# A hand-planned FFT kernel: where a copied spectrum's next step stands in TensorE's order, and when the next layer's tables are loaded

## The chip, the cores and the metric

One core of a Trainium2 chip runs the whole program. The metric is the device time of one execution in microseconds (us). Of the kernel before there are three runs, with a median of 811.83 us, and one execution under the profiler.

## What is computed

The network applies two layers in turn, each twice: A, B, A, B on `x` of 2048 rows by 512 columns, all in float32.

```python
x = x + A(layernorm(x))     # irfft2(rfft2(x) * W): over both axes
x = x + B(layernorm(x))     # y = irfft(rfft(u, 2L) * rfft(K, 2L))[:L] + u * Dskip, per column, over the rows
x = x + A(layernorm(x))
x = x + B(layernorm(x))
# K[d, l] = Re sum_n C[d,n] * exp(dt[d] A[d,n] l) * dt[d] B[d,n]   (512 columns x 2048 steps, 128 states)
```

The kernel `K` and its spectrum are the same for both B layers, so they are computed once.

## The kernel before, in words

The Fourier transforms are matrix products in two steps, each with a small table, and with an elementwise step between. Layer B (`forward_b`, `group_b`, `inv_b`) works on halves of 256 columns, called e=0 and e=1, and on eight groups q=0 to 7 of frequencies in each half. For one half:

- `forward_b` (L795) normalizes, multiplies by the first table and sends the result through a DMA (L809) to the rows of a large SBUF buffer, `Y[:, 8192:]` for e=0 and `Ya` for e=1.
- `group_b` (L859) takes one group. It needs the spectrum of K for that group in a buffer `kh` (a ring of four). In most cases a DMA loads it from DRAM (L886). For e=1 of the first layer B it doesn't exist yet. There the group loads the half-transformed K (`yk`, L874, a ring of three) and a table (L875), TensorE makes the spectrum (L824, called by L878), ScalarE copies it to `kh` (L882), and a DMA on ScalarE's queue stores it to `khat` (L883) for the second layer B. I call this step K. Then comes step X: the spectrum of the signal (L824 again, called by L891), which reads neither `kh` nor the store. After it come the product on VectorE (L898), the sums on GpSimd (L904), the inverse step V on TensorE (L915) and the copy back on ScalarE (L924).
- `inv_b` (L927) loads the rows again, transposed, by a DMA within SBUF (L934), after all eight groups of its half, multiplies (L942) and adds to `x` (L948).

In the second half of layer B's groups (e=1) the loads of `inv_b` for e=0 run at the same time. Once they are through, `Y[:, 8192:]` is free, and the ring `G` there holds tables for the second layer A: `first_a(1, 0)` loads its two with L666 and L668, `group_a` for g=1 to 15 with L594 and L596. All these go through the queue of SyncE (SP), which issues in program order and stops at an instruction whose wait isn't over.

Ahead of all that, `turn_k` (L1186) does the first step of K's own transform in 16 pieces: it loads from `kd` (L1193), multiplies (L1208), and for each of two halves ScalarE copies out of PSUM (L1213) and issues a store to `yk` (L1216). Twelve pieces lie beside the computation of K in the first part of the program. The last four lie beside layer B's e=0 groups; there each half takes a PSUM buffer of kind x (of which there are four) and a buffer of ring `iy` (four, shared with `forward_b`).

The order of instructions on each engine comes from a planner, `Clock` (L195 to L398). Every function above is a generator, a piece, that yields what its next step needs: engines, buffers, events. The planner keeps a model of when each engine, buffer and transfer is free, takes the earliest step that is ready (within 0.1 us the one of lowest rank), lets it emit its instructions, and moves on. What it emits is a fixed program; on the chip each engine runs its own list in order, and semaphores hold back what is not ready. Four details matter here:

- After a step, the piece's next step is ready no earlier than the end of everything that the step emitted, landings of DMAs included (L390 and L392). The model of a landing is 2.0 us behind the bytes at a fixed rate (L39, L302).
- A yield that begins with "+" leaves that time as it was (L391): the next step counts from the step before.
- `emitted(key, n)` asks only that n events of that name are in the program already, whatever their time; `after(key, n)` also takes their time.
- `mark` notes an event at the end of the step in which it stands. `("turn", 1)` marked eight times lets the first K step of e=1 load.

```python
            if not (isinstance(needs, str) and needs[:1] == "+"):
                p[2] = end
```

Of the kernel before, what the change touches and what calls it, by code (L numbers as in the profile page):

```python
# [400 lines left out]
class Net:  # L401
# [185 lines left out]
    def group_a(self, g):  # L587

        nc = self.nc
        Y1 = self.folded(1, g // 4)[:, :, :, g % 4]  # L590
        yield "SP G", self.emitted(("loaded", 0, 0 if g < 4 else 1), 8)
        G = self.w("G", [128, 1798])
        ca = G[:, :768].rearrange("p (a b) -> p a b", a=6)
        nc.sync.dma_start(ca, self.io["cGa"][g])  # L594
        W = G[:, 768:1796].rearrange("p (r s f) -> p r s f", r=2, s=2)
        nc.sync.dma_start(G[:, 768:1798], self.io["W"][g])  # L596
        yield "PE p:t AB", self.after(("forward", 1), 16), self.emitted(("loaded", 0, 1), 8)
        p = self.psum("t")
        AB = self.w("AB", [128, 2, 258])
        self.fold_d(p, 1, g)  # L600
        yield "POOL"
        nc.gpsimd.memset(AB[:, :, 0:65:64], 0.0)
        yield "ACT"

        re, im = slice(0, 64), slice(64, 128)
        pc, ps = p[:, 0:256], p[:, 256:512]
        for lanes, i in ((re, 0), (im, 1)):
            nc.scalar.copy(AB[lanes, i, 0:64], pc[lanes, 0:64])
            nc.scalar.copy(AB[lanes, i, 65:257], pc[lanes, 64:256])
        nc.scalar.copy(AB[im, 0, 1:257], ps[re])  # L610
        nc.scalar.mul(AB[re, 1, 1:257], ps[im], -1.0)
        self.drop(p)
        yield "POOL V"
        V = self.w("V", [128, 2, 258])
        nc.gpsimd.tensor_tensor(V[:, 1, :257], AB[:, 0, :257], AB[:, 1, :257], op=OP.subtract)
        yield "+ DVE"
        nc.vector.tensor_tensor(V[:, 0, :257], AB[:, 0, :257], AB[:, 1, :257], op=OP.add)
        self.drop(AB)
        yield "PE p:x p:x"
        X = [self.psum("x")[:, :257] for sg in range(2)]  # L620
        for sg in range(2):
            nc.tensor.matmul(X[sg], ca[:, sg, :], V[:, sg, :257], start=True, stop=True)
        self.drop(V)
        yield "DVE t1a t2a"
        t1, t2 = (self.w(k, [128, 2, 258]) for k in ("t1a", "t2a"))
        for sg in range(2):
            nc.vector.tensor_tensor(t1[:, sg, :257], X[sg], W[:, 0, sg], op=OP.mult)
            nc.vector.scalar_tensor_tensor(t2[re, sg, :257], X[sg][im], -1.0, W[im, 1, sg], op0=OP.mult, op1=OP.mult)
            nc.vector.tensor_tensor(t2[im, sg, :257], X[sg][re], W[re, 1, sg], op=OP.mult)
        self.drop(*X)  # L630
        yield "POOL Za"
        Z = self.w("Za", [128, 2, 258])
        nc.gpsimd.tensor_tensor(Z[:, :, :257], t1[:, :, :257], t2[:, :, :257], op=OP.add)
        self.drop(t1, t2)
        yield "PE p:h tp"
        tp = self.w("tp", [128, 2, 64])
        v = self.psum("h").rearrange("p (b m) -> p b m", b=4)
        H = [ca[:, 2 + 2 * sg:4 + 2 * sg, :].rearrange("p r (s c u) -> p r s c u", s=16, c=2)[:, :, :, 0] for sg in range(2)]
        for b in range(2):
            for sg in range(2):  # L640
                for r, o in ((0, 65 * b), (1, 65 * b + 1 - b)):
                    nc.tensor.matmul(v[64 * r:64 * r + 64, b], Z[:, sg, o:o + 64], ca[:, 2 + 2 * sg + r, :],
                                     start=sg == 0, stop=sg == 1)
        for sg in range(2):
            nc.tensor.matmul(v[:, 2 + sg], Z[:, sg, 129:257], H[sg], start=True, stop=True)
        self.drop(Z, G)
        yield "ACT", self.emitted(("fold", 1), g // 4 * 4)
        nc.scalar.copy(Y1[:, 0:2], v[:, 0:2].rearrange("p b (s m) -> p b s m", s=16))
        P, M = (v[:, 2 + sg].rearrange("p (r s u) -> p r s u", r=2, s=16) for sg in range(2))
        yc, ys = Y1[:, 2:4, :, 0:4], Y1[:, 2:4, :, 4:8]  # L650
        tp = tp.rearrange("p r (s u) -> p r s u", s=16)
        nc.scalar.copy(tp, P)
        yield "DVE"
        nc.vector.tensor_tensor(yc, tp, M, op=OP.add)
        nc.vector.tensor_tensor(ys[:, 0], M[:, 1], tp[:, 1], op=OP.subtract)
        nc.vector.tensor_tensor(ys[:, 1], tp[:, 0], M[:, 0], op=OP.subtract)
        self.mark("group", 1)

    def first_a(self, r, g):

        nc = self.nc
        Y1 = self.folded(r, g // 4)[:, :, :, g % 4]
        yield "SP G", self.emitted(("loaded", 0, 0), 8) if r else self.after(("norm", 0), 16)
        G = self.w("G", [128, 1284])
        ca = G[:, :768].rearrange("p (a b) -> p a b", a=6)
        nc.sync.dma_start(ca, self.io["cPa"][g])  # L666
# [192 lines left out]
    def group_b(self, r, q, e):  # L859
# [10 lines left out]
        kh = self.w(ring, [128, 2, 2, 256])  # L870
        self.mark("kh")
        if new:
            y, gk = self.w("yk", [128, 2, 2, 256]), self.w("gk", [128, 2, 4, 32])
            nc.sync.dma_start(y.rearrange("p g h d -> p g (h d)"), self.yk[1, two].rearrange("g c a b h d -> (c a b) g (h d)"))  # L874
            nc.sync.dma_start(gk, self.io["cGk"][q])  # L875
            yield "PE p:x p:x"
            K = [self.psum("x") for _ in range(2)]
            self.spectrum(gk, [y[:, j] for j in range(2)], K)  # L878
            self.drop(gk, y)
            yield "ACT"  # L880
            for j in range(2):
                nc.scalar.copy(kh[:, j].rearrange("p r d -> p (r d)"), K[j])  # L882
            nc.scalar.dma_start(self.khat[:, two, :, d], kh)  # L883
            self.drop(*K)
        else:
            nc.sync.dma_start(kh, self.khat[:, two, :, d])  # L886
        Y = self.place[e][:, two].rearrange("p g (h d) -> p g h d", h=2)
# [298 lines left out]
    def turn_k(self, q, i):  # L1186

        nc = self.nc
        kd = self.kd[q].rearrange("j (a s) d -> a j (s d)", s=16)
        last = q == 3  # L1190
        yield "SP yk" if last else "SP KT", self.after(("stored", q))
        KT = self.w("yk" if last else "KT", [128, 4, 128])
        nc.sync.dma_start(KT, kd[:, :, 128 * i:128 * i + 128])  # L1193
        if i == 0:
            yield "SP gk" if last else "SP sk"
            sk = self.w("gk" if last else "sk", [1, 128])
            nc.sync.dma_start(sk, self.io["B_Dskip"].rearrange("(q a d) -> q a d", q=4, a=1)[q])
            yield "DVE"
            o = KT[0:1, :, 0:32]
            nc.vector.tensor_tensor(o, o, sk.rearrange("p (j d) -> p j d", j=4), op=OP.add)  # L1200
        yield "PE p:x p:x" if last else "PE p:k"
        if last:
            p = [self.psum("x") for _ in range(2)]
        else:
            p = self.psum("k")
            p = p[:, :512], p[:, 512:]
        for h in range(2):
            nc.tensor.matmul(p[h], self.Rk[:, h, :], KT.rearrange("p j m -> p (j m)"), start=True, stop=True)  # L1208
        self.drop(KT)
        for h in range(2):  # L1210
            yield "ACT iy" if last else "ACT yh"
            r = self.w("iy" if last else "yh", [128, 4, 128])
            nc.scalar.copy(r.rearrange("p s (j d) -> p s j d", j=4), p[h].rearrange("p (j s d) -> p s j d", j=4, s=4))  # L1213
            if last:
                self.drop(p[h])
            nc.scalar.dma_start(self.yk[q // 2, :, :, :, i, h, 128 * (q % 2):128 * (q % 2) + 128]  # L1216
                                .rearrange("g c a d -> (g c) a d"), r)
            self.drop(r)
        self.mark("turn", q // 2)

    def plan_k(self):
# [195 lines left out]
```

## Time and profile before

| | us |
|---|---|
| three runs: lowest, median, highest | 807.78, 811.83, 815.23 |
| the profiled execution | 816.34 |
| its span, first to last instruction | 814.5 |

The span falls into parts, by the first and last instructions of the lines: the computation of K and the first layer A up to about 360 us; layer B, half e=0, to about 439 us; half e=1 to 512 us; then its inverse step, the second layer A to about 690 us, and the second layer B to the end. A row of the timeline reads: start in us, duration, engine, line, operation, output and input, count, and in brackets the idle time before it and what ended it. A row of the stage view reads: the stage, its length, busy time of TensorE's matmuls and weight loads, of VectorE, ScalarE and GpSimd, then the granted clock, the DMA engines' share and the rate. A row of the waits reads: who waited for whom, us in total, times, longest.

### The profile page before, as it was taken

The page shows a single profiled execution, that of the slowest core. Times are in us where ns is not written, and L with a number is a line of the kernel's source. Part 1 is how long each engine was busy: PE and PEld are TensorE (multiplying, and loading weights), DVE is VectorE, ACT ScalarE, POOL GpSimd, SP SyncE. Part 2 cuts the span into 40 slices and gives each one's busy share as a digit, 9 for nine tenths or more (in the row PEclk, how much of TensorE's full clock was granted, in tenths as well). Part 3 has the DMA queues.
Part 4 walks back from the last instruction along what each step waited for, and adds up shares of the span by engine and source line. Part 5 has one row for each costly group of instructions (what it writes and reads, how often), then busy time and mean ns, then how long its engine had stood idle before and what let it go on. Part 6 is the DMA issues. An engine that isn't in the chain of part 4 may idle for free. (4 is left out here: it accounts for less than half of the span.)

```text
span 814.5 us, 23463 instructions
## 1 busy us (share of the span) xinstructions
PE 657.6 (81%) x9892; PEld 421.9 (52%) x9892; DVE 511.9 (63%) x1019; ACT 423.7 (52%) x771; POOL 308.3 (38%) x339
## 2 busy tenths in 40 slices
PE   4388888778799898798778776899887898788896
PEld 4377555445556443346323542677765554444565
DVE  5957477947947684973333624686777598375632
ACT  5676898878877667744234132266543233423120
POOL 4381345625615231400323134255443454074520
PEclk9699899989899999999898988999998899989999
DMA  9424312531524844369967984710665424765938
GB/s 331 143 79 134 108 46 99 169 97 67 173 64 161 282 131 142 126 230 219 273 175 203 290 267 177 204 50 1 225 215 175 145 55 105 171 183 149 280 87 277
DMA packets 87544, 132.51 MB, mean 163 GB/s; under 512 B 5804, under 2 KB 59824, under 8 KB 86800
## 3 DMA queue, kind: packets, MB, share of 16 engines
q1 hardware_dynamic: 53008, 93.26, 37.7%
q10 hardware_dynamic: 34432, 37.76, 16.5%
q8 instruction: 78, 1.28, 0.7%
q14 instruction: 26, 0.21, 0.1%
HBM read 70.31 MB, written 27.13 MB: 120 GB/s over the span
## 5 line engine op out<-in xcount | busy, mean ns | idle before, releaser
L1151 POOL TENSOR_TENSOR Y<-wk,Y 128x1024 f32<-128x1024 f32 x32 | 66.2, 2069 | 116.3 <-issue 64.8
L904 POOL TENSOR_TENSOR wk<-wk 128x512 f32<-128x512 f32 x32 | 40.0, 1275 | 124.1 <-DVE wk L898 97.3
L898 DVE TENSOR_TENSOR wk<-ps,Y 128x512 f32<-128x512 f32 x64 | 39.5, 683 | 54.4 <-DMA Y<-khat 14.7
L942 PE MATMUL ps<-wk,cRbT 64*128 64x256 f32 x512 | 61.9, 384 | 7.1 <-DVE x L948 2.6
L793 ACT COPY wk<-ps 128x512 f32<-128x512 f32 x64 | 37.0, 587 | 57.9 <-PE ps L791 45.6
L791 PE MATMUL ps<-wk,cRb 128*32 128x256 f32 x1024 | 61.8, 388 | 5.5 <-DVE wk L514 3.1
L1136 DVE SCALAR_TENSOR_TENSOR wk<-wk,ps 128x1024 f32<-128x1024 f32 x32 | 38.9, 1216 | 38.6 <-ACT wk L1134 38.5
L942 PEld LDWEIGHTS ps<-wk,cRbT 64*128 64x128 f32 x512 | 51.7, 187 | 17.4 <-issue 7.2
L557 PE MATMUL ps<-cRa,wk 128*128 128x256 f32 x128 | 37.9, 423 | 27.6 <-POOL wk L539 26.8
L915 PE MATMUL ps<-wk,Y 32*32 32x256 f32 x1344 | 41.2, 433 | 21.1 <-POOL wk L904 13.4
L898 DVE TENSOR_TENSOR Y<-ps,wk 128x512 f32<-128x512 f32 x64 | 39.6, 683 | 27.0 <-issue 19.9
L1104 PE MATMUL ps<-wk,Y 96*128 96x512 bf16 x128 | 42.0, 412 | 17.0 <-DMA yk<-wk 7.1
L948 DVE TENSOR_TENSOR x<-x,ps 128x256 f32<-128x256 f32 x64 | 24.9, 409 | 48.6 <-PE ps L942 48.5
L791 PEld LDWEIGHTS ps<-wk,cRb 128*32 128x32 f32 x1024 | 37.9, 111 | 30.6 <-issue 5.7
L1120 ACT ACTIVATE Y<-ps 128x1024 f32<-128x1024 f32 x48 | 46.1, 1027 | 8.5 <-PE ps L1104 8.3
L924 ACT COPY Ya<-ps 128x256 f32<-128x256 f32 x64 | 19.4, 385 | 57.7 <-PE ps L915 44.5
L740 PE MATMUL ps<-cDaT,apart 128*32 128x256 f32 (+1 forms) x256 | 47.3, 333 | 1.4 <-DVE x L768 1.2
L1147 DVE TENSOR_TENSOR Y<-ps,Y 128x1024 f32<-128x1024 f32 x32 | 39.0, 1219 | 13.6 <-ACT ps L1140 13.5
L1164 PEld LDWEIGHTS ps<-Y 128*32 128x32 f32 x2048 | 34.4, 120 | 23.4 <-issue 15.4
L539 POOL TENSOR_TENSOR wk<-wk 128x256 f32<-128x256 f32 x32 | 27.1, 846 | 51.0 <-ACT wk L512 45.2
L904 POOL TENSOR_TENSOR wk<-Y 128x512 f32<-128x512 f32 x22 | 27.5, 1278 | 46.9 <-DVE Y L898 42.7
L1164 PE MATMUL ps<-Y 128*32 128x64 f32 x2048 | 39.7, 236 | 6.6 <-ACT wk L744 4.8
(216 smaller groups left out, 1668.9 us busy)
## 6 DMA issues: line engine op xcount, KB each, us to landing
yk<-wk ACTq DMA_DIRECT2D x32, 256.0 KB, 2.7
wk<-khat SPq DMA_DIRECT2D x16, 512.0 KB, 7.4
Y<-in_W_dram SPq DMA_DIRECT2D x12, 515.0 KB, 4.4
x<-in_cPa_dram SPq DMA_DIRECT2D x16, 384.0 KB, 3.5
Y<-in_cGa_dram SPq DMA_DIRECT2D x12, 384.0 KB, 3.1
x<-in_W_dram SPq DMA_DIRECT2D x16, 258.0 KB, 3.8
x<-in_A_x_dram SPq DMA_DIRECT2D x8, 512.0 KB, 6.9
kd<-wk SPq DMA_DIRECT2D x4, 1024.0 KB, 9.7
```

The lines of the kernel that those rows point to most:

```text
L740: nc.tensor.matmul(p[32 * i:32 * i + 32, o:o + n], self.folded(r, i)[:, b, s2].rearrange("p g m -> p (g m)"), self.DaT[:, b, first:first + ...
L791: self.nc.tensor.matmul(p[o:o + 32, 256 * h:256 * h + 256], self.Rb[:, 2 * h + j, 32 * a:32 * a + 32], xn[s], start=True, stop=True)
L898: nc.vector.tensor_tensor(t[c][:, j], x, kh[:, j, ::-1, :] if c else kh[:, j], op=OP.mult)
L904: nc.gpsimd.tensor_tensor(Z[:, :, c], t[0][:, :, c], t[1][:, :, c], op=op)
L915: nc.tensor.matmul(v[j][h][i:i + 32], gi[o:o + 32, j, 4 + 2 * s + c, :], Z[o:o + 32, j, c, :], start=c == 0, stop=c == 1)
L942: nc.tensor.matmul(q[s], self.RbT[o, i, :], y[o, i, :], start=i == 0, stop=i == 3)
L1104: self.nc.tensor.matmul(p, f[:, c:c + 128], self.oh[:k, o:o + 512], start=True, stop=True)
L1120: nc.scalar.activation(m[:, :, 1024:] if i == 2 else m[:, i, :1024], p.rearrange("p (i m) -> p i m", i=2) if i == 2 else p, AF.Exp)
L1136: nc.vector.scalar_tensor_tensor(s, c, MAGIC, p, op0=OP.subtract, op1=OP.subtract)
L1147: nc.vector.tensor_tensor(E[:, 1, :1024], p, m[:, :1024], op=OP.mult)
L1151: nc.gpsimd.tensor_tensor(E[:, 0, :1024], c, m[:, :1024], op=OP.mult)
L1164: nc.tensor.matmul(pk[32 * j:32 * j + 32, 64 * e:64 * e + 64], E1[:, r, i, :], E2[:, r, i], start=r == 0, stop=r == 1)
```

## The change

Three edits. The first two concern when steps become ready in the planner; the third the order of loads. No computation, transfer or buffer is added or taken away.

1. In `group_b`, a `yield "+"` behind the store to `khat`. Step X of the group is then ready from the end of step K's matmuls on, where it was ready from the landing of the store on.
2. In `turn_k`, a `yield "+"` behind each store to `yk`. The second half's copy is ready from the end of the matmuls on, where it waited for the first half's landing. The mark of the event `turn`, too, now carries the time of the matmuls' end. The semaphores on the chip still wait for the stores.
3. The first four table sets of the second layer A (`first_a(1, 0)` and `group_a` for g=1, 2, 3) wait until 16 `kh` buffers have been taken, so until the loads of the last group of e=1 are in the program. Before, they waited for eight `loaded` events, so for the last load of `inv_b` for e=0.

```diff
@@ group_a
-        yield "SP G", self.emitted(("loaded", 0, 0 if g < 4 else 1), 8)
+        yield "SP G", (self.emitted("kh", 16) if g < 4 else self.emitted(("loaded", 0, 1), 8))
@@ first_a
-        yield "SP G", self.emitted(("loaded", 0, 0), 8) if r else self.after(("norm", 0), 16)
+        yield "SP G", self.emitted("kh", 16) if r else self.after(("norm", 0), 16)
@@ group_b
             nc.scalar.dma_start(self.khat[:, two, :, d], kh)
             self.drop(*K)
+            yield "+"
         else:
             nc.sync.dma_start(kh, self.khat[:, two, :, d])
@@ turn_k
             nc.scalar.dma_start(self.yk[q // 2, :, :, :, i, h, 128 * (q % 2):128 * (q % 2) + 128]
                                 .rearrange("g c a d -> (g c) a d"), r)
             self.drop(r)
+            yield "+"
         self.mark("turn", q // 2)
```

## The prediction

> **What bounds the kernel now.** I read the page first, then the busy time by stage around the change.
>
> ```profile
> PE 657.6 (81%) x9892; PEld 421.9 (52%) x9892; DVE 511.9 (63%) x1019; ACT 423.7 (52%) x771; POOL 308.3 (38%) x339
> ```
> ```profile
> 360.00:439.00 79.00, 64.41 (x1216) 34.20 (x1214) 34.10 (x71) 30.48 (x65) 17.55 (x14) 0.96 0.84 208
> 439.00:512.00 73.00, 52.30 (x1201) 28.02 (x1196) 28.74 (x54) 20.37 (x55) 22.47 (x18) 0.86 0.76 237
> 512.00:560.00 48.00, 43.80 (x300) 35.48 (x296) 38.72 (x100) 23.15 (x54) 23.26 (x34) 1.00 0.40 108
> ```
>
> TensorE (PE) bounds the program on average, at 81%. The middle row is e=1 of the first layer B, the stage that edits 1 and 3 touch: PE is busy 52.3 of 73 us (72%), against 82% in the stage before and 91% in the one behind. No engine is full there, nor are the DMAs, so it waits on itself. Three timelines say where: SP's queue, PE and VectorE (DVE).
>
> ```profile
> 439.18 0.36 SPq L874 DMA_DIRECT2D wk<-yk  x1
> ...
> 448.75 2.13 SPq L875 DMA_DIRECT2D wk<-in_cGk_dram  x1
> 452.87 5.58 SPq L934 DMA_DIRECT2D wk<-Y  x2
> 473.70 0.35 SPq L666 DMA_DIRECT2D Y<-in_cPa_dram  x1
> ...
> 475.74 0.43 SPq L874 DMA_DIRECT2D wk<-yk  x1
> ...
> 485.80 0.33 SPq L875 DMA_DIRECT2D wk<-in_cGk_dram  x1
> 512.44 7.22 SPq L934 DMA_DIRECT2D wk<-Ya  x4
> ```
> ```profile
> SPq L666 <- DMA wk<-Y: 15.1, 1, 15.1
> SPq L874 <- DMA yk<-wk: 5.8, 1, 5.8
> ```
> ```profile
> 444.62 3.94 PE L824 MATMUL ps<-wk 64*32 64x256 f32 x64 [0.66 <-DMA wk<-in_cGk_dram]
> ...
> 460.26 1.09 PE L824 MATMUL ps<-Ya,Y 64*32 64x256 f32 x32
> 461.15 1.07 PE L824 MATMUL ps<-wk 64*32 64x256 f32 x32
> ...
> 480.22 2.40 PE L915 MATMUL ps<-wk,Y 32*32 32x256 f32 x64 [4.08 <-POOL wk L904]
> 482.55 4.44 PE L824 MATMUL ps<-wk 64*32 64x256 f32 x86
> ...
> 493.28 2.40 PE L915 MATMUL ps<-wk,Y 32*32 32x256 f32 x64 [4.05 <-POOL wk L904]
> 496.62 1.96 PE L824 MATMUL ps<-wk 64*32 64x256 f32 x32 [0.94 <-ACT Ya L924]
> ```
> ```profile
> 461.91 5.02 DVE L898 TENSOR_TENSOR wk<-ps,Y 128x512 f32<-128x512 f32 x8
> ```
>
> Two things are seen. First, step K of groups 0 and 1 (input wk) runs at 444.62, yet step X of group 0 (input Ya) only at 460.26, and so the first product at 461.91. X needs no store; it simply stands that late in PE's list. Second, SP stops for 15.1 us at L666, a table of the next layer A, until the transposed loads have finished reading the place it goes to. Behind it in the queue stand the K loads of groups 4 to 6 (from 475.74), so their step K runs at 482.55, and group 7's at 496.62. The loads for the half's inverse can only start at 512.44.
>
> **Edit 1: X behind K.** Adds nothing, moves X of eight groups. K of group 0 ends about 446.7, X takes 1.09, so the first product can start at about 448.4, behind ScalarE's copy, instead of 461.91: 13.5 us earlier. What X passes is `inv_b`'s matmuls (L942), which then run among the groups, and they count in full below. New risk: X ahead of V (L915) in the list costs V 1.1 us each time, nothing in sum.
>
> **Edit 3: tables behind the last K loads.** Four pairs of DMAs leave their place ahead of groups 4 to 7. Group 4's load is next held by its `kh` buffer, until the store of group 0 has landed (issues of this stage with their size and time to landing, then the store's issue):
>
> ```profile
> wk<-yk SPq DMA_DIRECT2D x8, 512.0 KB, 4.8
> khat<-Y ACTq DMA_DIRECT2D x8, 512.0 KB, 12.1
> wk<-in_cGk_dram SPq DMA_DIRECT2D x8, 128.0 KB, 6.1
> ```
> ```profile
> 448.39 0.85 ACTq L883 DMA_DIRECT2D khat<-Y  x1
> ```
>
> That is 448.4 + 12.1 = 460.5 instead of 475.74, 15 us earlier. Group 7 waits for group 3's store: its table lands at 448.75 + 6.1 = 454.9, K and copy take 2.2, the store 12.1, so its loads go at about 469.2 and land at 475.3; in the trace they landed at 485.8 + 6.1 = 491.9. Neither limit is the end of the stage, then; PE or the DMAs are.
>
> *DMAs.* The stage moved this much:
>
> ```profile
> 439.00:475.00 36.00, 28.61 (x585) 16.82 (x578) 16.41 (x34) 9.68 (x26) 10.01 (x8) 0.91 0.89 252
> 475.00:512.00 37.00, 23.69 (x619) 11.20 (x618) 12.33 (x20) 10.69 (x30) 12.47 (x10) 0.82 0.63 221
> ```
> ```profile
> 480.00:490.00 10.00, 8.21 (x192) 4.14 (x192) 0.70 (x2) 4.34 (x10) 1.39 (x2) 0.70 1.00 377
> ```
>
> By 475 it had moved 36 x 252 = 9.1 MB. What K of group 7 still needs is four loads of 640 KB and three stores of 512 KB, 4.2 MB; at the 377 GB/s of the third row that is 11 us, to 486; at 252 it is 16.7 us, to 491.7. The way of one group from K to its copy back is K 1.1, copy 1.2, product 2.5, sums 2.5, V 2.4, copy 1.2 us, 10.9 in all (K, V and the product from the rows above, half of 5.02; the copies as two of 0.59, the L1213 rows below; the sums from this row of GpSimd):
>
> ```profile
> 507.97 2.50 POOL L904 TENSOR_TENSOR wk<-wk 128x512 f32<-128x512 f32 x2 [0.21 <-DVE wk L898]
> ```
>
> So the DMAs allow an end of 497 to 502.6, against 512.4.
>
> *PE.* 52.3 us of work from 439.2 on, and 3.7 us of the last group in which PE has nothing else (sums and copy back), give 495.2 without any wait: 17.2 us at most. With the share of the stage before (82%), 52.3/0.82 = 63.8, 503.0: 9.4 us. I take the middle, 86.5%: 60.5 us, the end at 499.7, a gain of **12.7 us** (9.4 to 17.2), within what the DMAs allow. The stage behind is 91% PE and hides nothing, so the gain passes on.
>
> The tables themselves:
>
> ```profile
> Y<-in_W_dram SPq DMA_DIRECT2D x12, 515.0 KB, 4.4
> Y<-in_cGa_dram SPq DMA_DIRECT2D x12, 384.0 KB, 3.1
> ```
>
> At most four pairs of 0.9 MB, 3.7 MB. With the change they go at about 470 to 485, and the layer that uses them starts past 560 us; the cover is 70 us. If it were gone, they would cost 3.7 MB / 252 GB/s = 14.6 us.
>
> [...]
>
> **Edit 2, first part of the program.** Twelve turns; each holds one of three large PSUM buffers until its second copy, which the planner sets behind the first one's landing. The rows are the landing of the stores of L1216 in this part, and PE's waits there:
>
> ```profile
> DMA to landing us min/median/max: 2.6/2.6/3.4
> ```
> ```profile
> PE ps L1104 <- DMA yk<-wk: 7.1, 2, 4.4
> PE ps L1104 <- ACT wk L1213: 4.5, 3, 3.8
> ```
>
> Side by side the copies free the buffer sooner. Upper bound: both PE waits vanish, 11.6 us. Lower bound: with two copy buffers, the next turn's copy meets a store that hasn't landed, and ScalarE stands; a landing of 2.6 us at each of 12 turns is a loss of 31 us. Between these I take the row of PE's waits as nearer, since the planner reckons with the landing, but only a sixth of it, since ScalarE and PE share that part: **2 us** gained.
>
> **Edit 2, beside e=0.** The four last turns hold two of four x buffers, for instance one from its copy at 403.39 to that at 419.45:
>
> ```profile
> 403.39 0.59 ACT L1213 COPY wk<-ps 128x512 f32<-128x512 f32 x1 [1.14 <-DMA Ya<-wk]
> ...
> 419.45 0.59 ACT L1213 COPY wk<-ps 128x512 f32<-128x512 f32 x1 [0.60 <-ACT wk L1213]
> ```
> ```profile
> DVE wk L898 <- ACT wk L1213: 12.3, 3, 6.1
> ```
> ```profile
> 414.64 18.56 SPq L809 DMA_DIRECT2D Ya<-wk  x2
> ```
>
> Upper bound 12.3 us, the product's waits for these copies. But the earlier mark lets the planner put the first K loads on SP ahead of the last row store (L809, issued at about 432.7). SP would then stand there until the turns' stores land (the 5.8 us above, to 439.18), and the row store, which X of all groups needs, would follow three pairs of loads, at about 442: 9 us later, the lower bound. Nearest is the wait of 5.8 that stays either way; I take **1 us** gained.
>
> **Sum.** 12.7 + 2 + 1 = 15.7. The profiled execution took 816.34 us, so 800.6 for such a one; the median of the three runs is 811.83, 0.6% below it, so I predict **796 us**.
>
> **The rivals.**
> [...]
> - *Tables collide with the inverse's loads.* SP issues them just ahead of L934. If group 7's loads go late, near the 485.8 of now, the 14.6 us of tables lie before the loads that the next stage waits for, and the gain is given back: 15.7 - 14.6, **811 us**. For it: SP is one queue, and those loads now start 26.6 us behind group 7's. Against: group 7's own limit of 469. [...]
> - *It does nothing.* The planner fills the freed places with `inv_b`, and the products start no sooner: **809 us**, edit 2's gain alone. Against: a group and the `inv_b` of its number have the same rank (L1324, L1326), and X would be ready first.
> - *Slower: ScalarE stands at the turns.* Place: the 24 copies of the first part, in a stage where ScalarE is the busiest engine beside PE (behind the stage and its length: PE, weight loads, DVE, ScalarE):
>
> ```profile
> 140.00:200.00 60.00, 47.32 (x684) 29.58 (x683) 42.29 (x61) 48.87 (x59) 27.59 (x19) 0.91 0.37 115
> ```
>
>   If every second copy stops ScalarE for a landing of 2.6 us, 12 x 2.6 = 31 us are lost against 13.7 gained: **829 us**. It decides from (13.7 + 8.1)/24 = 0.9 us of standing per copy on. For it: ScalarE runs its list in the planner's order, and edit 2 makes the planner think less of landings. Against: today's waits there are small:
>
> ```profile
> ACT wk L1213 <- DMA khat<-wk: 4.6, 2, 3.0
> ```
>
> **How the numbers follow.** Forecast 0.52 (its own range 784 to 803), full clock 0.10, collision 0.16, nothing 0.07, slower 0.15. The range of 784 to 814 holds all but the slower case and a few hundredths below: 784 is both upper bounds of the largest terms, 17.2 + 11.6, about, and 814 lies past the collision. A measurement of this kernel can tell about 1%, 8 us, from no change: faster 0.62 (the first two), same 0.23, slower 0.15.
>
> **What would show it.** Right: an X step (input Ya) within 3 us of the first K step, the first product of e=1 before 452; no wait of SP's at L666 ahead of a K load; group 4's load 10 us or more nearer the first one; the stage from the first K load to the inverse's first load (73 us now) at 57 to 64. Wrong: that stage over 70; the inverse's first matmul (L942) of e=1 over 15 us behind its first load; ScalarE's waits at L1213 over 15 us; or a first part (to the first L824) that shifted by more than 8 us.

## The result

The changed kernel is slower: 824.66 us, median of four runs (819.16 to 835.04), against 812.71 for four of the kernel before; the ratio is 1.0107 [1.0062, 1.0152]. The forecast was 796, with 814 as its upper end. The profiled execution took 824.54 us, its span 822.8. One kernel's times spread over some 15 us on the same chip (the kernel before from 808.97 to 824.86 on one), so below a ratio says how a kernel stands, and a trace, which is one execution, says why. Comparisons leave disturbed runs out; for one experiment (turns_ranked_later) that left two of twelve, so there I compare the medians.

Behind L884 the changed kernel's lines are numbered one higher: the product L899, the sums L905, V L916, the inverse's loads L935, the turns' copies L1214. First the page's busy times, which say nothing: the same work, in a longer span.

```profile
PE 658.1 (80%) x9892; PEld 423.5 (51%) x9892; DVE 509.6 (62%) x1019; ACT 425.1 (52%) x772; POOL 306.7 (37%) x339
```

The view by stage says more. The first fence is the kernel before, the second the changed one; the columns are those of the stage view in the prediction.

```profile
140.00:360.00 220.00, 186.88 (x2803) 105.61 (x2802) 153.86 (x258) 164.28 (x201) 81.61 (x57) 0.94 0.48 152
```
```profile
140.00:360.00 220.00, 178.92 (x2678) 101.17 (x2673) 143.44 (x242) 162.86 (x196) 80.41 (x57) 0.92 0.43 137
441.00:520.00 79.00, 57.91 (x1373) 32.26 (x1364) 30.33 (x56) 24.80 (x66) 23.49 (x19) 0.89 0.86 245
```

In the same 220 us of the first part TensorE has done 8.0 us less (178.92 against 186.88) and VectorE 10.4 us less, and the first layer B's first step (L791) starts at 368.4 us instead of 360.6, 7.8 us later. From there to the first K load the changed kernel needs 73.1 us against 78.6, so 5.5 us of this come back. But the stage from the first K load to the inverse's first load, the second row, is longer: 441.49 to 520.46, 79.0 us against 73.3. TensorE is busy for 73% of it, as it was before (72%), at a granted clock of 0.89 instead of 0.86. Part of that is work that has moved: 5.4 us of forward products (L791, from 441.77) now lie behind the first K load. From there to the end the two kernels agree within 1 us (302.3 and 302.1). The span's loss of 8.3 us is about what the first part lost; the two stages behind it nearly cancel.

The same three timelines as in the prediction, of the changed kernel: SP, TensorE and VectorE.

```profile
441.49 0.36 SPq L874 DMA_DIRECT2D wk<-yk  x1
...
443.87 1.40 SPq L875 DMA_DIRECT2D wk<-in_cGk_dram  x1
445.32 1.55 SPq L809 DMA_DIRECT2D Ya<-wk  x2
...
465.03 3.35 SPq L874 DMA_DIRECT2D wk<-yk  x1
...
487.93 1.26 SPq L875 DMA_DIRECT2D wk<-in_cGk_dram  x1
494.06 0.35 SPq L666 DMA_DIRECT2D Y<-in_cPa_dram  x1
...
520.46 3.35 SPq L935 DMA_DIRECT2D wk<-Ya  x3
```
```profile
458.75 2.27 PE L916 MATMUL ps<-wk,Y 32*32 32x256 f32 x51 [3.01 <-issue]
461.89 3.25 PE L824 MATMUL ps<-Ya,Y 64*32 64x256 f32 x64 [0.87 <-DMA Ya<-wk]
...
474.62 1.79 PE L824 MATMUL ps<-Ya,Y 64*32 64x256 f32 x21 [2.59 <-issue]
...
496.04 1.50 PE L824 MATMUL ps<-Ya,Y 64*32 64x256 f32 x21 [3.37 <-issue]
```
```profile
464.04 4.88 DVE L899 TENSOR_TENSOR wk<-ps,Y 128x512 f32<-128x512 f32 x8 [20.38 <-PE ps L824]
```

Three things are seen. The tables (L666) stand behind the K loads, and SP's stop of 15.1 us at L666, ahead of group 4, is gone, as meant. The row stores (L809), which step X reads, are now issued behind three pairs of K loads, so X starts at 461.89, held last by `DMA Ya<-wk`: 20.4 us behind the first K load, hardly better than the 21.1 before. The late rows also give SP a new stop: the inverse's loads for e=0 (L935) stand until the row stores have landed, and group 4's load stands behind them, at 465.03.

```profile
SPq L935 <- DMA Ya<-wk: 10.4, 1, 10.4
```

And TensorE has gaps marked "issue", in which it waited for nothing that the profile shows.

### The profile page after: what moved, and what is told of

It is laid out like the page before. It is cut to its first block, busy times and chain, and to the rows that moved or that the text cites. A ratio compares the mean times of both kernels' runs of the same rounds, so it can differ in the third digit from the quotient of the medians.

```text
span 822.8 us, 23478 instructions
## 1 busy us (share of the span) xinstructions
PE 658.1 (80%) x9892; PEld 423.5 (51%) x9892; DVE 509.6 (62%) x1019; ACT 425.1 (52%) x772; POOL 306.7 (37%) x339
## 5 line engine op out<-in xcount | busy, mean ns | idle before, releaser
L905 POOL TENSOR_TENSOR wk<-wk 128x512 f32<-128x512 f32 x32 | 39.9, 1272 | 118.4 <-DVE wk L899 114.9
L899 DVE TENSOR_TENSOR wk<-ps,Y 128x512 f32<-128x512 f32 x64 | 39.5, 683 | 65.2 <-PE ps L824 46.6
L791 PE MATMUL ps<-wk,cRb 128*32 128x256 f32 x1024 | 61.9, 388 | 3.5 <-DVE wk L514 2.8
L899 DVE TENSOR_TENSOR Y<-ps,wk 128x512 f32<-128x512 f32 x64 | 39.6, 683 | 29.3 <-issue 21.1
L916 PE MATMUL ps<-wk,Y 32*32 32x256 f32 x1344 | 39.7, 429 | 16.7 <-POOL wk L905 7.3
L791 PEld LDWEIGHTS ps<-wk,cRb 128*32 128x32 f32 x1024 | 38.9, 111 | 27.2 <-issue 4.7
L761 PE MATMUL ps<-wk,cRaT 128*128 128x512 f32 x64 | 36.1, 656 | 11.3 <-ACT wk L744 6.5
```

The source lines that it names most:

```text
L761: nc.tensor.matmul(q, self.RaT, Y4, start=True, stop=True)
L791: self.nc.tensor.matmul(p[o:o + 32, 256 * h:256 * h + 256], self.Rb[:, 2 * h + j, 32 * a:32 * a + 32], xn[s], start=True, stop=True)
L899: nc.vector.tensor_tensor(t[c][:, j], x, kh[:, j, ::-1, :] if c else kh[:, j], op=OP.mult)
L905: nc.gpsimd.tensor_tensor(Z[:, :, c], t[0][:, :, c], t[1][:, :, c], op=op)
L916: nc.tensor.matmul(v[j][h][i:i + 32], gi[o:o + 32, j, 4 + 2 * s + c, :], Z[o:o + 32, j, c, :], start=c == 0, stop=c == 1)
```

## The experiments

Fifteen kernels, each beside the kernel before on its chip. The first four try the theory that edit 2 carries the loss. In each expectation A is the theory that it tries, and B, or "rival", the other one.

**One edit, or two.** Each diff is against the changed kernel.

groups_and_tables (edits 1 and 3; edit 2 taken out):

```diff
@@ turn_k
             self.drop(r)
-            yield "+"
```

> Edits 1 and 3 without edit 2 (no change in turn_k). Theory A (edit 2 loses, edits 1 and 3 gain as forecast): the first part, to the first L791 at 360.6 us, and the e=0 half stay as they were (within 2 us); the first X of e=1 comes within 5 us of the first step K, since the last row stores stay where they were (issued at 433 and 436); the stage from the first K load to the inverse's first load takes 58 to 66 us, not 73, and the whole is 7 to 14 us faster than before. Theory B (the stage is held by its stores, row loads and PE's order, whatever is moved): the first X comes early, but the stage takes 70 to 76 us, and the time is within 4 us of before.

Measured: 811.94 us, ratio 0.9949 [0.9913, 0.9985]. It beats both kernels, by less than I said.

turns_alone (edit 2 alone):

```diff
@@ group_b
             self.drop(*K)
-            yield "+"
@@ group_a
-        yield "SP G", (self.emitted("kh", 16) if g < 4 else self.emitted(("loaded", 0, 1), 8))
+        yield "SP G", self.emitted(("loaded", 0, 0 if g < 4 else 1), 8)
@@ first_a
-        yield "SP G", self.emitted("kh", 16) if r else self.after(("norm", 0), 16)
+        yield "SP G", self.emitted(("loaded", 0, 0), 8) if r else self.after(("norm", 0), 16)
```

> Edit 2 alone (both copies of a turn without regard to the landing, the event turn at the matmuls' end). Theory A: this carries the loss. First part 7 to 12 us longer (first L791 at 368 to 372), the last row stores of e=1 behind the first K loads on SP as in the changed kernel (at 445 or later), the whole 8 to 16 us slower than before. Theory B: the first part loses only what another order of the same work loses by chance; the whole within 4 us of the changed kernel's 12 us loss only if the e=1 stage loses too; without edits 1 and 3 it would keep its 73 us, and the time lies 0 to 6 us above before.

Measured: 839.01 us, 1.0296 [1.0237, 1.0355]. Alone it costs 24 us, more than expected. In its trace the first part is 5.6 us late (L791 at 366.2), and most of the loss lies in the stage behind the first K load, which takes 91.0 us (439.78 to 530.78) instead of 73.3. Beside edits 1 and 3 the same edit costs less, 1.6%: the edits don't simply add up.

groups_alone (edit 1) and tables_alone (edit 3) leave out `turn_k`'s line as well, and the first keeps `group_b`'s line without the conditions, the second the conditions without the line:

```diff
@@ turn_k, in both
             self.drop(r)
-            yield "+"
@@ group_b, in tables_alone
             self.drop(*K)
-            yield "+"
```

> Edit 1 alone (X behind K in TensorE's order; tables still ahead of the K loads of groups 4 to 6, no change in turn_k). Theory A: the first X and first product come 10 us or more sooner, SP still stops at L666 for 10 us or more, and about half of the gain is had: 3 to 8 us faster than before. Theory B: no gain, within 3 us of before.

> Edit 3 alone (tables behind the last K loads; X still placed behind the store's landing, no change in turn_k). Theory A: SP no longer stops at L666 ahead of a K load, group 4's load comes 10 us or more sooner, the end of the stage 3 to 8 us sooner, the whole 3 to 8 us faster. Theory B: group 4's load comes sooner, but its step K doesn't come sooner by more than 4 us, as TensorE's order waits for other things; the whole within 3 us of before.

Measured: 817.79 us, 1.0010 [0.9969, 1.0051], and 829.93 us, 1.0173 [1.0107, 1.0238]. Edit 2 carries the loss; that edits 1 and 3 gain singly was wrong. Edit 3 needs edit 1, and the TensorE timeline of tables_alone shows why (L915 is step V, L824 step X):

```profile
503.22 2.40 PE L915 MATMUL ps<-wk,Y 32*32 32x256 f32 x64 [4.07 <-POOL wk L904]
505.55 1.71 PE L824 MATMUL ps<-Ya,Y 64*32 64x256 f32 x32
511.42 2.39 PE L915 MATMUL ps<-wk,Y 32*32 32x256 f32 x64 [4.17 <-POOL wk L904]
513.75 2.02 PE L824 MATMUL ps<-Ya,Y 64*32 64x256 f32 x32
519.77 2.40 PE L915 MATMUL ps<-wk,Y 32*32 32x256 f32 x64 [4.00 <-POOL wk L904]
```

Without edit 1, X is ready only when a store is reckoned to have landed. The late groups then come out as blocks, X, product, sums, V, one behind the other, each with 4 us in which TensorE waits for GpSimd's sums: a period of 8.3 us for some 4.2 of matmuls. The kernel before has two such waits (4.08 and 4.05), tables_alone the three here in a row, groups_and_tables none over 2.7. TensorE's waits for those sums from 436 to 532 us are the measure, first groups_and_tables, then tables_alone; the kernel before has 12.2 us of them and groups_alone 13.5, so edit 1 by itself doesn't take them away either:

```profile
PE ps L916 <- POOL wk L905: 5.1, 5, 2.7
```
```profile
PE ps L915 <- POOL wk L904: 21.5, 11, 4.2
```

**Which turns, and which half of the edit.** In these diffs `last` marks the four turns beside e=0, and `h` the half of a turn's spectrum.

```diff
-            yield "+"
+            if not last: yield "+"     turns_first_part
+            if last: yield "+"         turns_last_four
+            if h == 0: yield "+"       release_after_first_half
```
```diff
-            yield 2 * b, self.forward_b(0, b, 1, sb)
+            yield -1, self.forward_b(0, b, 1, sb)      late_rows_first
```

> The changed kernel with the turned spectra's early release only for the turns of the first part (the last four turns, beside the second half's forward products, wait for the landing of their store again); the other two edits stay. Theory A, the planner's order: the early release moves the first part's work, so the first load of the first part's end (L824) comes about 8 us later than before, and the second half's stage is that of groups_and_tables, 68 us: about 4 us over the kernel before, a ratio near 1.005. Rival, the loss lies in the last turns alone: the first part still ends late, but the time is given back, ratio 0.995.

Measured: 824.69 us, 1.0077 [1.0035, 1.0120].

> The changed kernel with the early release only for the last four turns; the other two edits stay. Theory A: the first part is that of the kernel before within 2 us, the stretch from there to the first K load is about 5 us shorter, and the first X of the second half's groups is about 13 us later behind that load than in groups_and_tables (22 instead of 7), since the row stores L809 stand behind K loads on SP: a stage near 79 us, in all 0 to 3 us over the kernel before, ratio 0.999 to 1.004. Rival, that X is late because of the first part's shift: X within 10 us of the first K load and a ratio of 0.99.

Measured: 815.38 us, 0.9991 [0.9945, 1.0036]. Its trace has the first K load at 429.4 and X at 448.0: 18.6 us behind, against 7.3 in groups_and_tables (438.9, 446.2). So X is 11 us late, and the earlier start of the stage pays for most of it.

> The changed kernel with the early release only after the first half of a turned spectrum's store, so that the planner's mark of a finished turn again holds the landing, while the second half's copies still follow at once; the other two edits stay. Theory A1, the early mark moves the loads and so the order: the first part and the stage are those of groups_and_tables, ratio 0.995. Theory A2, the copies placed side by side hold the buffers and the engines: the first part stays 8 us late as in the changed kernel, ratio 1.005 to 1.01.

Measured: 822.32 us, 1.0076 [1.0037, 1.0114], with the first part as late as in the changed kernel (L791 at 367.0): A2, it is the copies side by side that cost, not the early mark.

> The changed kernel with one number of the planner's rank changed: the second half's forward products for the second e go ahead of everything that is ready, so that their row stores are not placed behind K loads. Theory A, the late rows hold the second half's groups: the first X comes near 446 us instead of 462, and the stage is 68 us instead of 79, some 8 to 11 us less than the changed kernel, a ratio to the kernel before near 1.000. Rival, the stage is held by its loads and TensorE's fetches: X comes earlier and the stage's end stays, within 3 us of the changed kernel, ratio 1.01.

Measured: 819.72 us, 1.0033 [0.9992, 1.0074]. The sum is near what was expected, the step is not: X came at 459.4, still 11.7 behind the first K load, since its last row stores were still issued at 442 to 449 us (its trace is of its slowest execution, 825.36). What the late rows cost by themselves stays at turns_last_four's reading.

Against groups_and_tables the first part's turns cost 1.3% (10 us) and the last four 0.4% (3 us); together 1.7%, and the changed kernel lies 1.6% above it. Within intervals of some 0.4% for each ratio the two terms add up; the last four's 0.4% alone is not clear of nothing.

**Why the first part loses.** The early release for one quarter of the spectra (the index q of `turn_k`), with edits 1 and 3, and a control without it:

```diff
+            if q == 0: yield "+"       turn_first_quarter; q == 1 and q == 2 for the two others
```
```diff
-                    yield 4 * b + 6 + i, self.turn_k(b // 2, i)
+                    yield 4 * b + 7 + i, self.turn_k(b // 2, i)      turns_ranked_later, with no "+" in turn_k
```

> groups_and_tables with the early release for the four turns of the first quarter of the spectra alone (q = 0 of the four). Theory A, one place: the whole 8 us of the first part's loss come from one of the quarters, and this kernel shows all of it (the second layer B's first forward product, L791, near 368 us, ratio 1.005) or none of it (near 359 us, ratio 0.995). Theory B, a dense order: each quarter that is released early displaces the work on ScalarE and TensorE a little, 2 to 4 us each, and this kernel starts L791 near 361 us.

> As turn_first_quarter, for the second quarter's four turns alone (q = 1). Theory A: all or none of the 8 us; theory B: 2 to 4 us.

> As turn_first_quarter, for the third quarter's four turns alone (q = 2), whose copies stand beside layer A's inverse. Theory A: all or none of the 8 us; theory B: 2 to 4 us. Where the three quarters' losses add up to the 8 us, B is right; where one of them has it all, A.

> A control without any early release: groups_and_tables with the turns' rank in the planner one higher (4b + 7 + i instead of 4b + 6 + i), so that their steps are placed a little later among the same other steps. If any small displacement of the first part's dense order costs several us, whatever it is (theory B's ground), L791 starts 3 to 10 us later than in groups_and_tables and the ratio is 1.000 to 1.008; if the early release costs by what it does itself (copies that follow each other at once), this control stays within 2 us of groups_and_tables, ratio 0.995.

Measured: 0.9990 [0.9956, 1.0025], 1.0030 [0.9996, 1.0064] and 1.0069 [1.0031, 1.0107], so 0.4, 0.8 and 1.2% above groups_and_tables. Neither theory fits: the third quarter alone has about the whole 1.3%, the first is not clear of nothing, and the three add up to nearly twice what all together cost. The control's median is 814.10 against 816.21, 0.3% above groups_and_tables (two of its twelve executions lie far below the others, 798.47 and 805.36; those two alone give 0.983): another place for the turns costs little. So it is the release. Which quarter pays is not explained: ScalarE's waits for stores to `yk` in the three traces, 3.8, 5.3 and 0.6 us, don't follow the losses. (The profiled execution of the third quarter was the fastest of its twelve, 814.41 with a median of 820.87, so its trace doesn't show the loss.)

What the release does on ScalarE is in its timeline, in the changed kernel: four copies of two turns, in tiles of a ring of two (`yh`), each followed by its store.

```profile
216.90 0.62 ACT L1214 COPY wk<-ps 128x512 f32<-128x512 f32 x1
217.55 0.52 ACTq L1217 DMA_DIRECT2D yk<-wk  x1
218.17 0.59 ACT L1214 COPY wk<-ps 128x512 f32<-128x512 f32 x1 [0.65 <-PE ps L1165]
218.78 0.52 ACTq L1217 DMA_DIRECT2D yk<-wk  x1
...
220.42 0.58 ACT L1214 COPY wk<-ps 128x512 f32<-128x512 f32 x1
221.03 0.52 ACTq L1217 DMA_DIRECT2D yk<-wk  x1
223.76 0.59 ACT L1214 COPY wk<-ps 128x512 f32<-128x512 f32 x1 [2.76 <-DMA yk<-wk]
```

The fourth copy, whose tile's last store went out at 218.78, stands 2.76 us for that store's landing, and everything behind it on ScalarE stands too. Over the stretch from 140 to 375 us the waits at the turns are, in the kernel before (TensorE's for the turns' stores and copies, ScalarE's for the stores), and in the changed one:

```profile
PE ps L1104 <- DMA yk<-wk: 7.1, 2, 4.4
...
ACT wk L1213 <- DMA khat<-wk: 4.6, 2, 3.0
PE ps L1104 <- ACT wk L1213: 4.5, 3, 3.8
...
ACT wk L1213 <- DMA yk<-wk: 0.6, 1, 0.6
```
```profile
ACT wk L1214 <- DMA yk<-wk: 7.6, 5, 2.8
...
PE ps L1105 <- ACT wk L1214: 6.3, 5, 2.0
...
PE ps L1209 <- ACT wk L1214: 3.6, 2, 1.8
...
ACT wk L1214 <- DMA khat<-wk: 2.6, 2, 1.9
```

ScalarE's waits for the turns' stores go from 0.6 to 7.6 us; with those for the stores of K's finished spectra to `khat` (L845), which share the ring, from 5.2 to 10.2. TensorE's waits for the copies go from 4.5 to 9.9, but its 7.1 us for the stores themselves are gone, so its direct waits at the turns are even a little less than before (9.9 against 11.6). These rows alone therefore don't add up to 8 us: they show where ScalarE stands, not the whole price. How long a landing takes stands in the list of DMA issues (count, size, median us from issue to landing):

```profile
yk<-wk ACTq DMA_DIRECT2D x24, 256.0 KB, 2.8
```

The store that the fourth copy waited for took 4.9 us, the longest of them; the shortest took 2.6 us.

Whether the two tiles matter can be tried without touching the release: give the ring four tiles, for which the work buffer has room.

```diff
-RING1 = {... "yh": (512, 2), ...}
+RING1 = {... "yh": (512, 4), ...}
```

The rest of the three kernels is the changed one, turns_first_part, and groups_and_tables.

> The changed kernel with four tiles instead of two in the ring (yh) from which the turned spectra's copies of the first part take their place; nothing else. Theory A, the two tiles: copies that follow each other at once need the tile whose store has not landed; with four tiles the waits of L1213 for stores to yk in the first part fall from 7.6 us to under 1.5, L791 starts near 360 us instead of 368, and the ratio is that of turns_last_four, 0.996 to 1.001. Theory B, the order: the waits fall but L791 stays within 2 us of 368 and the ratio near 1.010.

Measured: 813.37 us, 0.9965 [0.9924, 1.0006]. In the trace no copy of a turn waits for a store in the first part any more, and TensorE has the lost work back (the stage view from 140 to 360 us, then what is left of TensorE's waits for the copies):

```profile
140.00:360.00 220.00, 187.87 (x2836) 105.58 (x2836) 153.18 (x261) 165.03 (x202) 81.24 (x57) 0.95 0.48 150
```
```profile
PE ps L1105 <- ACT wk L1214: 3.6, 3, 1.8
```

187.87 us against 178.92 with two tiles and 186.88 before; L791 starts at 355.0 instead of 368.4.

> turns_first_part (early release in the first part alone, and the other two edits) with four tiles in the ring yh. Theory A: the ratio falls from 1.008 to that of groups_and_tables, 0.993 to 0.998. Theory B: it stays at 1.005 to 1.010.

> groups_and_tables (no early release) with four tiles in the ring yh, as the control for the two others. Theory A: without the release few copies wait for a store to yk (0.6 us in the first part), but the third spectra's copies (L844) take their tiles from the same ring, so a gain of up to 3 us is possible: ratio 0.991 to 0.996. Theory B says the same here; a gain over 5 us would say that the ring was the limit with or without the release.

Measured: 0.9948 [0.9915, 0.9982] and 0.9975 [0.9936, 1.0014]. The first falls from 1.0077 to the ratio of groups_and_tables, as theory A said. The deeper ring alone brings nothing (0.9975 against 0.9949, within both intervals), though I had allowed it 3 us. So the loss of the first part is the release together with two tiles; neither alone costs.

Two things these runs don't separate. The planner reckons with the tiles, too, so four of them change the planned order as well as the waits on the chip, and the order of ScalarE's instructions differs between the two kernels. And the granted clock goes along with the times: its mean over the executions is 0.928 in turns_first_part against 0.933 for the kernel before beside it, and 0.938 against 0.932 in ring4_first_part. How much of the 10 us is standing and how much is clock is open.

## Why the prediction was wrong, point by point

- **Edit 2, first part: the step that failed.** I took +2 us, "since the planner reckons with the landing", between a gain of 11.6 and a loss of 31. It was a loss of 10 us, by the mechanism of the lower bound, which was also the slower rival: with two tiles the next copy meets a store that hasn't landed, and with four tiles the loss is gone. Each bound came true in part. Of TensorE's 11.6 us of waits the 7.1 for the stores went, but the 4.5 for the copies became 9.9. And 5 copies stood for 7.6 us in all, not 12 for 2.6 each. What I held against it, today's small waits at L1213, was no evidence: those for the turns' own stores (0.6 us) were small because the second copy had been kept behind the landing, which is what the edit took away. My test for it, over 15 us of waits of ScalarE at L1213, came out at the line: 10.2 us for stores, 15.6 with its waits for TensorE there, against 5.2 and 6.5 before. The other test, a shift of the first part of over 8 us, was the clear one: the first step X of e=0 went from 387.2 to 398.6. The rival's 829 us was nearer than the forecast; it supposed 0.9 us of standing per copy as its point of decision, and less sufficed because the gain on the other side failed too.
- **Edit 2, beside e=0.** I took +1 us, between +12.3 and -9, the latter by the row stores behind the K loads. The latter happened; the former mostly did not. In turns_last_four the product still waits 10.3 us for one of these copies (12.3 for three in the kernel before). The early mark does bring the first K load sooner, 69.8 us behind L791 against 80.4 in groups_and_tables, but X then came 11 us later behind that load, 18.6 us instead of 7.3. In sum it is a loss of 3 us [0.4% with 0.6% either way], not clear of nothing, so a value near nothing came close by luck: its ground, "the wait of 5.8 that stays either way", was not what decided it.
- **Edits 1 and 3.** The path is right: in groups_and_tables X starts 7.3 us behind the first K load instead of 21.1, SP's stop at L666 is gone, and the blocks are, too. The size is wrong: 0.5%, 4 us [1 to 7], for 12.7. In its trace the stage has 67.7 us, where I had 60.5. TensorE's wait without a releaser ("issue") in it is 8.4 us, against 1.7 before (the rows are below). Those 6.7 us are most of what is missing, by the trace; no run took them away, so this is read and not tried. The chain for group 7 also left out the ring `yk`: I had its loads wait for group 3's store and go at 469.2, but they stood for one of the three tiles of `yk` until K of group 4 had run at 483.64, and went at 484.9. I also counted edit 3 as a gain by itself, and it is a loss of 1.7% without edit 1.
- **Full clock, collision, nothing.** Full clock was the case of this stage at a granted clock of 1.00; that closed gaps would bring it was my assumption, and no run shows it. The granted clock of the stage rose only from 0.86 to 0.89, and the time did not follow: the stage went from 73.3 to 79.0 us. From 439 to 512 us the clock was 0.78 in tables_alone, with TensorE 67% busy, 0.86 in the kernel before with 72%, and 0.91 in the changed kernel with 77%; which of the two follows the other was not tried. The tables did not collide: they went out at 494 to 498 us, and the inverse's loads of the changed kernel then waited last for the last group's copy back on ScalarE, behind 5.0 us in which SP stood for a load of the tables:

```profile
SPq L935 <- ACT Ya L925: 17.0, 1, 17.0
```

  "It does nothing" was wrong: X does move, where its rows are there.
- **The chance.** I gave the slower side 0.15, though the lower bounds of the two terms of edit 2 (31 and 9 us) were together more than twice the upper bound of edits 1 and 3 (17.2), each with a mechanism of its own. A value chosen near the upper rows on both made a small plus out of the two riskiest terms.

## What to carry to other kernels

A step that waits for a landing may be the thing that keeps a short ring from being overrun: before taking the wait out, count the tiles in the ring against the steps that will now follow each other, and add tiles in the same edit (here the ratio is 1.0077 with two tiles and 0.9948 with four). When an order is planned, releasing one step also moves what other queues issue next, so ask which store falls behind which load (here a row store on SP, from about 432.7 to 445.3 us). And two edits on the same path can have a sign only together: edit 3 loses by 1.7% alone and gains with edit 1.

## What the runs showed that I had not expected

TensorE's gaps marked "issue" are larger in this stage than they were. From 436 to 532 us the waits are, in the kernel before, the changed one, and groups_and_tables:

```profile
PE ps L915 <- issue: 1.0, 2, 0.6
...
PE ps L824 <- issue: 0.7, 1, 0.7
```
```profile
PE ps L824 <- issue: 7.4, 3, 3.4
...
PE ps L916 <- issue: 3.0, 1, 3.0
```
```profile
PE ps L824 <- issue: 6.3, 2, 5.1
...
PE ps L916 <- issue: 2.1, 2, 1.6
```

In the changed kernel the gap before 474.62 us is one of them. The two microseconds from 472 to 474 hold one packet of a queue of kind "instruction", among the others:

```profile
q1 hardware_dynamic: 149, 0.31, 77.1%
q10 hardware_dynamic: 35, 0.10, 24.2%
q8 instruction: 1, 0.02, 3.0%
```

It is one packet of 0.02 MB. All four gaps of over 0.5 us in the changed kernel here have such a packet 2.1 to 2.8 us before TensorE goes on, although there is only one in about 7 us (12 from 436 to 520 us); the longest gap in groups_and_tables, 5.09 us up to 472.84, has one between 470 and 471.5 us. That TensorE waits for its own instructions there is my guess from this and was not shown: the trace doesn't say which engine a packet is for. In the example 0.31 MB of loads went over SP's queue in the same two microseconds. From 140 to 360 us the changed kernel has 21 such packets with 0.34 MB, and its waits list one gap marked "issue" there, of 0.8 us, so a packet does not always go with a gap. Busy DMA engines alone don't explain the gaps: they are 0.83 busy in the changed kernel from 436 to 532 us, with 10.4 us of such gaps, and 0.84 in the kernel before from 360 to 436 us, with 1.8. A kernel with fewer transfers in this stage, which could tell more, wasn't run.
